# Float64 w_in lands bank by bank in the decoded weights' own buffers, w_out in two landing buffers, under a new step list

## The chip, the cores and the metric

One core of a Trainium2 chip runs the whole program. The time is device microseconds of one execution on that core; the median of several executions counts. PE is the matmul engine, DVE the vector engine, ACT the scalar engine, POOL the GpSimd engine, and SP only issues DMAs.

## What is computed

```python
# attention: B, H, S, D = 4, 8, 768, 48 (r, k, v, w, u in float32)
for t in range(S):
    cur = einsum('bhd,bhe->bhde', u[None] * kt, vt)
    y[:, :, t] = einsum('bhd,bhde->bhe', rt, state + cur)
    state = wt[:, :, :, None] * state + einsum('bhd,bhe->bhde', kt, vt)
x = y.transpose(0, 2, 1, 3).reshape(3072, 384)
# first MoE: w_in (384 x 2048) and w_out (2048 x 384) come in float64
h = x @ w_in
g = h * cos(h)
x2 = g @ w_out
# second MoE: phi (384 x 32), 8 experts w1 (384 x 1024), w2 (1024 x 384), float32
logits = x2 @ phi        # softmax over the tokens for dispatch, over the slots for combine
out = c @ slot_out       # slot_out from 8 experts of 4 slots each
```

## The kernel before

The 3072 tokens are worked in 24 blocks of 128. For each block j, the attention part runs the recurrence in chunks of 64 (loads `lw`, `lk`, `lr`, `lv`, `lz`; transposes `wT`, `kT`, `rT`, `kN` and matmuls `A`, `U`, `y` on PE; the scans `scan` and `sp`, the products `L` and `ks`, the masked copy `mask`, the state steps `z` and `st`, and `xl` on DVE; copies on ACT; `ru` and `D` on POOL). Its result is a block of x, held as a high and a low part. Then `h.t.q` multiplies block t by bank q of w_in (four banks of 512 columns, 9 matmuls each), and `turns`, `rest`, `cos` and `mul` make g from it: `turns` and `cos` on ACT, `rest` and `mul` on DVE. `gT`, `gc` and `l` transpose g and multiply it by w_out @ phi; the softmax steps (`sum` to `es`) follow per pair of blocks. After the last block the eight experts and the output run.

Both float64 weights are decoded on the chip before use. Each is cut in eight pieces of 256 columns or rows, of 768 KB. A piece is loaded by `raw`, and then needs one ACT step (`abs`) and three DVE steps (`d1`, `d2a`, `d2b`, lines 329, 334, 342), which leave a float32 tile. For a piece n of w_in, `whi` (ACT), `wn` (PE, lines 363 and 364) and `wc` (ACT) split it into the high and low part of bank n // 2, in the tile `wu{n // 2}`. For a piece of w_out, `oT`, `oc`, `om`, `pc`, `pT` and `ps` make its part of w_out @ phi.

Before, a piece of w_in lands in one of two buffers of the pool `raw`, except that the first piece is cut in two halves, the second of them landing in the buffer of bank 0. Four pieces of w_out land two by two in the buffers of banks 3 and 2, the other four in the pool `raw`. The decode tiles `a` have two buffers (pool `dec`).

The order is written out by hand in the string `HEAD`: a list of 1,896 steps, `name.argument.argument`. Each engine runs its own instructions in the order of that list, and nothing else moves them; SP too takes the DMAs in that order, so that a load whose buffer is not yet free holds back every load behind it. A step waits only for what it reads and for the buffers that it takes. The tiles that `wT`, `kT`, `rT`, `kN`, `A`, `U`, `y`, `wn`, `oT` and `pT` write in PSUM share three buffers (pool `ps_a`), those of `h` two (pool `ps_h`).

Of the kernel before, what the change touches and what calls it, by code (L numbers as in the profile page):

```python
# [871 lines left out]
wc.0.0 st.1.0 wn.0.1 d2b.o.1 z.1.1 abs.o.0 abs.o.2 rz.1.0 y.0 d1.o.0 st.1.1 wc.0.1 d2a.o.0 sr.2 oT.2 ru.2 oc.2 oT.3 xh.0 oc.3 d2b.o.0 rz.1.1 kT.2
d1.o.2 xl.0 oT.1 ks.2 lv.3 oT.0 sp.2 y.1 abs.i.1 oc.1 d2a.o.2 d1.i.1 oc.0 kN.2 d2b.o.2 wT.3 om.0 wf.3 xh.1 d2a.i.1 xl.1 oT.4 ksn.2 oT.5 oc.4 U.2
d2b.i.1 oc.5 z.2.0 raw.i.3 st.2.0 lw.5 whi.1 abs.i.4 z.2.1 bo.2 rT.2 bs.2 st.2.1 L.2 wn.1.0 wc.1.0 lz.3 d1.i.4 wn.1.1 wc.1.1 d2a.i.4 rz.2.0 oT.7
scan.3 A.2 abs.i.3 d2b.i.4 d1.i.3 lk.3 D.2 mask.2 d2a.i.3 raw.i.6 h.0.0 oc.7 whi.4 wn.4.1 d2b.i.3 rz.2.1 wc.4.1 kT.3 turns.0.0 wn.4.0 lw.4 whi.3 lr.3
pc.0 ru.3 abs.i.6 sr.3 raw.i.5 ks.3 wc.4.0 oT.6 sp.3 oc.6 d1.i.6 wn.3.0 rest.0.0 wc.3.0 wn.3.1 lk.4 d2a.i.6 rT.3 wT.4 d2b.i.6 wc.3.1 L.3 z.3.0 wf.4
whi.6 cos.0.0 h.1.0 abs.i.5 scan.4 pT.0 raw.i.7 turns.1.0 wn.6.1 d1.i.5 wc.6.1 wn.6.0 bo.3 wT.5 mul.0.0 wc.6.0 sr.4 d2a.i.5 h.0.1 abs.i.7 d2b.i.5 sp.4
whi.5 bs.3 lz.2 A.3 ps.0 turns.0.1 lr.4 rz.3.0 y.2 wf.5 D.3 xh.2 om.1 rest.1.0 d1.i.7 kN.3 cos.1.0 mask.3 ksn.3 wn.5.0 rest.0.1 cos.0.1 wc.5.0 wn.5.1
mul.1.0 raw.o.4 gT.0.0 wc.5.1 d2a.i.7 kT.4 xl.2 lz.4 d2b.i.7 mul.0.1 abs.o.4 whi.7 U.3 pc.1 ks.4 ru.4 raw.o.5 st.3.0 h.0.2 wn.7.0 d1.o.4 turns.0.2
z.3.1 gc.0.0 d2a.o.4 wn.7.1 rest.0.2 wc.7.1 st.3.1 h.1.1 rT.4 gT.0.1 cos.0.2 abs.o.5 wc.7.0 scan.5 turns.1.1 d2b.o.4 bo.4 lw.6 oT.8 oc.8 mul.0.2  # L880
rest.1.1 sr.5 kN.4 d1.o.5 h.0.3 bs.4 cos.1.1 L.4 mul.1.1 pT.1 rz.3.1 d2a.o.5 lk.5 ksn.4 gc.0.1 y.3 turns.0.3 h.1.2 rest.0.3 oT.9 xh.3 ps.1 cos.0.3
raw.o.7 lv.4 d2b.o.5 oT.11 gT.0.2 z.4.0 turns.1.2 oc.11 lr.5 oc.9 D.4 xl.3 oT.10 oc.10 A.4 rest.1.2 U.4 mul.0.3 l.0.0 sp.5 l.0.1 st.4.0 mask.4 abs.o.7
lw.7 lr.6 z.4.1 om.2 cos.1.2 pc.2 gc.0.2 raw.o.6 mul.1.2 abs.o.6 h.2.0 ru.5 gT.0.3 rz.4.1 rT.5 gc.0.3 pT.2 d1.o.6 h.1.3 ps.2 rz.4.0 d1.o.7 st.4.1 wT.6
# [120 lines left out]
```

## Time and profile before

| | us |
|---|---|
| median of 3 executions (516.99 to 518.56) | 517.7 |
| the profiled execution | 517.14 |
| its span, first to last instruction | 515.4 |
| PE busy in the span | 481.4 |
| DVE busy | 426.2 |
| ACT busy | 318.7 |
| POOL busy | 100.2 |

The span is what the trace shows; the 1.74 us between it and the execution's own time lie around the program. Busy times are unions over the instructions of an engine. The trace numbers time from the start of the span.

### The profile page before, as it was taken

The numbers are of one execution on the slowest core, as the hardware profiler recorded it, in microseconds if no ns is written. First come the engines' busy times: TensorE is split into PE (matmuls) and PEld (weight loads), VectorE is DVE, ScalarE is ACT, GpSimd is POOL, SyncE is SP. The second block draws the span as 40 slices with busy tenths as digits, with TensorE's granted clock in tenths as the row PEclk, the third lists the DMA queues.
The fourth block names the chain that finished last, engine by engine and source line by source line (L and its number), as shares of the span: only waits on it lengthen the run. The fifth ranks groups of instructions, "written<-read, shape, count | busy, mean of one in ns | idle before, by whom it ended". The sixth has DMA issues, their size and how long they took to land.

```text
span 515.4 us, 15516 instructions
## 1 busy us (share of the span) xinstructions
PE 481.4 (93%) x6515; PEld 378.3 (73%) x6515; DVE 426.2 (83%) x809; ACT 318.7 (62%) x703; POOL 100.2 (19%) x127
## 2 busy tenths in 40 slices
PE   3677899999999999999999999999999999998994
PEld 2445568887888878888877878878788787774573
DVE  4989999998988879999799899899878966674423
ACT  3276687776576676676656766657665756564421
POOL 2431221234212221221114112133120100002200
PEclk9989999999999999999999999999999999999997
DMA  9995968642633315025260341525130891289948
GB/s 208 313 191 139 198 166 203 139 66 45 100 67 68 59 36 93 18 51 76 48 108 4 62 73 23 108 48 95 25 56 17 350 369 39 102 294 336 400 174 269
DMA packets 146325, 67.47 MB, mean 131 GB/s; under 512 B 127184, under 2 KB 134352, under 8 KB 146256
## 3 DMA queue, kind: packets, MB, share of 16 engines
q1 hardware_dynamic: 146256, 66.49, 51.5%
q8 instruction: 51, 0.84, 0.7%
q14 instruction: 18, 0.15, 0.1%
HBM read 61.75 MB, written 4.72 MB: 129 GB/s over the span
## 4 chain that ended last, share of the span: by engine, by line
PE 53%; DVE 7%; ACT 3%; issue 1%
PE h L421 9%; PE h L423 8%; PE h L422 8%; PE gT L455 6%; PE l L470 3%; PE E L566 3%; PE A L193 2%; PE hps L754 2%; PE so L794 2%; PE y L267 2%; PE U L239 1%; DVE g L440 1%; PE o L827 1%; PE rT L134 1%; PE kT L134 1%; DVE lt L214 1%
## 5 line engine op out<-in xcount | busy, mean ns | idle before, releaser
L421 PE MATMUL h<-wu,x 128*128 128x512 f32 x288 | 121.4, 422 | 1.4 <-DVE g L448 1.3
L423 PE MATMUL h<-wu,x 128*128 128x512 f32 x288 | 113.2, 393 | 0.0
L422 PE MATMUL h<-wu,x 128*128 128x512 f32 x288 | 112.6, 391 | 0.0
L444 ACT ACTIVATE g<-g,half_pi 128x512 f32<-128x512 f32 (+1 forms) x97 | 69.2, 719 | 32.2 <-DVE g L440 31.6
L436 ACT ACTIVATE g<-h 128x512 int32<-128x512 f32 (+1 forms) x96 | 56.6, 595 | 51.8 <-PE h L423 41.9
L440 DVE SCALAR_TENSOR_TENSOR g<-g,h 128x512 f32<-128x512 int32 (+1 forms) x96 | 64.5, 675 | 18.0 <-ACT g L436 17.6
L448 DVE TENSOR_TENSOR g<-g,h 128x512 f32<-128x512 f32 (+1 forms) x96 | 64.7, 675 | 13.3 <-ACT g L444 12.3
L207 POOL TENSOR_SCALAR_AFFINE_SELECT lt<-bo 64x512 f32<-64x512 f32 x48 | 37.3, 778 | 159.4 <-ACT bo L230 89.6
L421 PEld LDWEIGHTS h<-wu,x 128*128 128x128 f32 x288 | 54.2, 188 | 16.5 <-issue 3.5
L461 ACT COPY gt<-gT 128x512 f32<-128x512 f32 x89 | 51.8, 585 | 19.1 <-PE gT L455 15.7
L423 PEld LDWEIGHTS h<-wu,x 128*128 128x128 f32 x288 | 54.0, 188 | 12.3
L422 PEld LDWEIGHTS h<-wu,x 128*128 128x128 f32 x288 | 54.4, 189 | 8.7
L455 PE MATMUL gT<-cs,g 128*128 128x128 f32 x384 | 57.5, 275 | 0.2
L162 POOL TENSOR_TENSOR ru<-rn,u_b 128x384 f32<-128x384 f32 x24 | 26.2, 1092 | 133.8 <-DMA rn<-in_r_dram 82.9
L455 PEld LDWEIGHTS gT<-cs,g 128*128 128x128 f32 x384 | 44.7, 141 | 8.2 <-issue 1.9
L214 DVE COPY_PREDICATED lt<-cs,A 64x512 f32<-64x512 uint32 x48 | 35.4, 737 | 1.6 <-POOL lt L207 0.3
L253 ACT COPY rzs<-z 64x192 f32<-64x192 f32 x96 | 33.4, 348 | 4.1 <-DVE z L248 3.0
L149 DVE TENSOR_TENSOR_SCAN qt<-wf,one_b 128x520 f32<-128x520 f32 x24 | 30.4, 1267 | 5.8 <-ACT wf L144 5.7
L178 DVE TENSOR_TENSOR lt<-rT,pt 64x512 f32<-64x512 f32 x48 | 32.8, 683 | 0.8 <-PE rT L134 0.2
L470 PE MATMUL l<-gt,p_sb 128*32 128x128 f32 x768 | 30.7, 276 | 0.3 <-DVE gt L461 0.3
L193 PE MATMUL A<-lt,ks 64*64 64x64 f32 x768 | 28.0, 224 | 3.0 <-DVE st_state L256 1.6
L157 DVE TENSOR_TENSOR_SCAN pt<-wf,ini_f 128x520 f32<-128x520 f32 x24 | 30.1, 1256 | 0.1
(167 smaller groups left out, 782.5 us busy)
## 6 DMA issues: line engine op xcount, KB each, us to landing
we<-in_moe_w_dram SPq DMA_DIRECT2D x16, 1536.0 KB, 9.6
rawi<-in_moe_w_in_dram SPq DMA_DIRECT2D x7, 768.0 KB, 5.0
wn<-in_w_dram SPq DMA_DIRECT2D x24, 192.0 KB, 4.4
kn<-in_k_dram SPq DMA_DIRECT2D x24, 192.0 KB, 4.0
rn<-in_r_dram SPq DMA_DIRECT2D x24, 192.0 KB, 3.9
vn<-in_v_dram SPq DMA_DIRECT2D x24, 192.0 KB, 3.8
...
```

What stands on the lines that cost most here:

```text
L193: nc.tensor.matmul(ps[64 - 64 * a:128 - 64 * a, s, :], lhsT=ks[k, s, :], rhs=L[k, a, s, :], start=True, stop=True)
L214: nc.vector.copy_predicated(out=lt[j % 2][h, a], mask=mask[h].bitcast(U32).unsqueeze(1).to_broadcast([64, NS, C]), data=ps[h])
L421: nc.tensor.matmul(half[:, f], lhsT=xh[:, c, :], rhs=wh, start=(c == 0), stop=False)
L422: nc.tensor.matmul(half[:, f], lhsT=xl[:, c, :], rhs=wh, start=False, stop=False)
L423: nc.tensor.matmul(half[:, f], lhsT=xh[:, c, :], rhs=wl, start=False, stop=(c == KD - 1))
L436: nc.scalar.activation(gt.bitcast(I32), hp, AF.Copy, bias=0.25, scale=1.0 / TWO_PI)
L440: nc.vector.scalar_tensor_tensor(out=gt, in0=gt.bitcast(I32), scalar=-TWO_PI, in1=hp, op0=ALU.mult, op1=ALU.add)
L444: nc.scalar.activation(gt, gt, AF.Sin, bias=half_pi[:, 0:1])
L448: nc.vector.tensor_tensor(out=gt, in0=gt, in1=hp, op=ALU.mult)
L455: nc.tensor.transpose(ps[:, m * 128:(m + 1) * 128], gt[:, m * 128:(m + 1) * 128], ident)
L461: (nc.vector.tensor_copy if n >= ATT and n % 8 in (1, 2, 5) else nc.scalar.copy)(gt_t[t, q], pend.pop(("gT", t, q)))
L470: nc.tensor.matmul(lps_t[g][32 * m:32 * m + 32, o:o + TB], lhsT=p_sb[:, 4 * q + m, :], rhs=gt[:, m * 128:(m + 1) * 128], start=first, stop ...
```

## The change

It does four things. The whole bank q of w_in now lands in the buffer of `wu{q}`, the tile of its decoded halves; the first bank comes as two loads of 256 columns, the other three as one load of 1.5 MB each. Since the decoded halves overwrite the raw bank, the first `whi` of a bank comes after both pieces of the bank have been decoded, and four decode tiles take the place of two. All eight pieces of w_out go through the two buffers of the pool `raw`. The first piece is no longer decoded in halves, which makes one `d1`, `d2a`, `d2b` of 768 columns out of two of 384. And the step list is another one, from its first step to its last.

```diff
-    dec = d_stack.enter_context(tc.tile_pool(name="dec", bufs=2))
+    dec = d_stack.enter_context(tc.tile_pool(name="dec", bufs=4))
...
+    def e_raw(x, n):
         if x == "i":
-            if hf:
-                raw_t[x, n, hf] = wu_p.tile([128, 4 * DM, 2], I32, tag="wu0", name=f"rawi{n}b")[:, 0:768, :]
-            else:
-                raw_t[x, n, hf] = raw_p.tile([128, 768, 2], I32, tag="raw", name=f"rawi{n}")
...
-            nc.sync.dma_start(dst, src)
-        elif n < 4:
-            t = wu_p.tile([128, 4 * DM, 2], I32, tag=f"wu{3 - n // 2}", name=f"rawo{n}")
...
+            q, f = n // 2, slice((n % 2) * 256, (n % 2) * 256 + 256) if n < 2 else slice(0, 512)
+            if q not in rawi_t:
+                rawi_t[q] = wu_p.tile([128, KD * 512, 2], I32, tag=f"wu{q}", name=f"rawi{q}").rearrange("p (k f) t -> p k f t", k=KD)
+            t = rawi_t[q]
+            src = w_in[:, q * 512 + f.start:q * 512 + f.stop].bitcast(I32).rearrange("(k p) f -> p k f", p=128)
+            nc.sync.dma_start(t.rearrange("p k f t -> p k (f t)")[:, :, 2 * f.start:2 * f.stop], src)
+            for i in (n,) if n < 2 else (n, n + 1):
+                raw_t[x, i] = t[:, :, (i % 2) * 256:(i % 2) * 256 + 256, :]
         else:
             t = raw_p.tile([128, 768, 2], I32, tag="raw", name=f"rawo{n}")
...
     def e_whi(n):
-        if n % 2 == 0:
+        if n // 2 not in wu:
             wu[n // 2] = wu_p.tile([128, 2, KD, 512], F32R, tag=f"wu{n // 2}", name=f"wu{n // 2}")
...
-lw.0 lk.0 raw.i.2 z.0.0 wT.0 lw.1 kT.0 wf.0 scan.0 raw.i.0.0 abs.i.2 ks.0 sr.0 sp.0 d1.i.2 d2a.i.2 wT.1 lr.0 misc kN.0 ru.0 wf.1 scan.1 ksn.0 d2b.i.2
+raw.i.0 abs.i.0 raw.i.1 lw.0 d1.i.0 lk.0 abs.i.1 wT.0 raw.i.2 lw.1 d2a.i.0 d2b.i.0 z.0.0 lr.0 d1.i.1 d2a.i.1 d2b.i.1 kT.0 wf.0 whi.1 scan.0 misc ks.0
```

On SP, the first loads of the program now stand like this (`rawi` is a piece or a bank of w_in, `wn`, `kn`, `rn`, `vn` are the loads `lw`, `lk`, `lr`, `lv` of a block; rows with neither sign are in both):

```order
-L999 UNCONDITIONAL_BRANCH
-L607 DMA cs<-in_const_dram 128x320
+L983 UNCONDITIONAL_BRANCH
+L591 DMA cs<-in_const_dram 128x320
+L300 DMA rawi_155<-in_moe_w_in_dram 128x3x512 x2
 L117 DMA wn_121<-in_w_dram 128x8x48
 L117 DMA kn_119<-in_k_dram 128x8x48
-L310 DMA rawi_157<-in_moe_w_in_dram 128x3x512
+L300 DMA rawi_170<-in_moe_w_in_dram 128x3x1024
 L117 DMA wn_122<-in_w_dram 128x8x48
-L310 DMA rawi_175<-in_moe_w_in_dram 128x3x256
 L117 DMA rn_117<-in_r_dram 128x8x48
```

The whole first bank of w_in moved ahead of the loads of block 0, and the whole second bank stands between block 0 and block 1.

On DVE, the rows up to the product `L` of block 4 (the row with two `lt`), before the change:

```order
L149 SCALAR_TENSOR_TENSOR qt_1018<-wf,one_b 128x520
L342 SCALAR_TENSOR_TENSOR wo_sb<-rawo_915,ao_936 128x768
L225 TENSOR_REDUCE bo_1023<-ru_961 128x2x4
L448 TENSOR_TENSOR g_2_981<-g_2_981,h_2_967 128x512
L440 SCALAR_TENSOR_TENSOR g_1_1020<-g_1_1020,h_1_994 128x512
L153 RECIPROCAL ini_f<-qt_1018 128x8
L329 TENSOR_SCALAR ao_1015<-ao_1015 128x768
L178 TENSOR_TENSOR lt_125<-rT_1004,pt_811 64x512 x2
```

And after it (lines 320, 326, 424 and 432 are the 334, 342, 440 and 448 of before):

```order
L326 SCALAR_TENSOR_TENSOR wo_sb<-rawo_900,ao_967 128x768
L225 TENSOR_REDUCE bo_1041<-ru_1036 128x2x4
L157 SCALAR_TENSOR_TENSOR pt_1055<-wf,ini_f 128x520
L285 TENSOR_TENSOR x_115<-y_1003,x_115 128x3x128
L432 TENSOR_TENSOR g_1_995<-g_1_995,h_1_973 128x512
L320 SCALAR_TENSOR_TENSOR ao_858<-rawo_831,ao_858 128x768
L424 SCALAR_TENSOR_TENSOR g_3_1081<-g_3_1081,h_3_1045 128x512
L326 SCALAR_TENSOR_TENSOR wo_sb<-rawo_831,ao_858 128x768
L178 TENSOR_TENSOR lt_125<-rT_1083,pt_1055 64x512 x2
```

The scan of block 5 (`qt_1018`) and its reciprocal have left this place for a later one; `xl` of block 3 (the row with `x_115`), a `mul`, a `rest`, and the `d2a` and `d2b` of piece 5 of w_out have come ahead of it.

On PE, the rows around the matmuls `A` of block 4, which read that `L`, before:

```order
L423 MATMUL h_2_1102<-wu_685,x_115 128x512
L375 MATMUL woT_1113<-cs,wo_sb 128x128 x3
L375 MATMUL woT_1124<-cs,wo_sb 128x128 x3
L455 MATMUL gT_2_1128<-cs,g_2_981 128x128 x4
L375 MATMUL woT_1145<-cs,wo_sb 128x128 x3
L193 MATMUL A_1151<-lt_125,ks_959 64x64 x16
```

And after:

```order
L407 MATMUL h_2_1102<-wu_449,x_115 128x512
L359 MATMUL woT_1124<-cs,wo_sb 128x128 x3
L193 MATMUL A_1135<-lt_125,ks_993 64x64 x16
```

Some transposes of w_out moved from just ahead of `A` to elsewhere; over all rows ahead of it, before has one `oT` more (`oT.10`) and after one `l` more (`l.0.0`), and the rest is the same set in another order.

## Rows read from the trace of the kernel before

**Rows 1.** The page, section 1: busy time and share of each engine.

```profile
PE 481.4 (93%) x6515; PEld 378.3 (73%) x6515; DVE 426.2 (83%) x809; ACT 318.7 (62%) x703; POOL 100.2 (19%) x127
...
PE   3677899999999999999999999999999999998994
```

**Rows 2.** Busy time by stretch, granted clock, DMA share, GB/s, for PE, PEld, DVE, ACT, POOL.

```profile
0.00:70.00 70.00, 48.13 (x504) 33.44 (x506) 61.15 (x90) 38.44 (x75) 19.66 (x35) 0.98 0.90 209
70.00:120.00 50.00, 49.91 (x792) 41.89 (x792) 47.72 (x81) 38.98 (x87) 15.43 (x16) 1.00 0.60 132
120.00:400.00 280.00, 278.52 (x3914) 226.40 (x3907) 251.43 (x493) 183.82 (x416) 57.14 (x64) 1.00 0.34 58
```

**Rows 3.** Timeline of PE: start, length, instruction; in brackets the idle time before it.

```profile
...
21.34 2.04 PE L363 MATMUL wl<-ai,cs 128*128 128x512 f32 x2 [1.59 <-DVE lt L178]
...
23.61 1.05 PE L134 MATMUL kT<-cs,kn 128*128 128x128 f32 x4
...
73.39 1.10 PE L363 MATMUL wl<-ai,cs 128*128 128x512 f32 x2
...
91.27 0.97 PE L193 MATMUL A<-lt,ks 64*64 64x64 f32 x26
...
101.25 0.60 PE L200 MATMUL kN<-cs,ks 128*128 128x128 f32 x4
```

**Rows 4.** Timeline of DVE, the same columns.

```profile
...
6.65 1.24 DVE L149 TENSOR_TENSOR_SCAN qt<-wf,one_b 128x520 f32<-128x520 f32 x1 [5.52 <-ACT wf L144]
...
14.92 0.81 DVE L329 TENSOR_SCALAR ai<-ai 128x384 int32<-128x384 int32 x1
...
18.11 1.78 DVE L248 TENSOR_TENSOR z<-st_state,qt 128x192 f32<-128x192 f32 x1
...
24.27 0.54 DVE L342 SCALAR_TENSOR_TENSOR ai<-rawi0b,ai 128x384 int32<-128x384 int32 x1
24.74 0.54 DVE L225 TENSOR_REDUCE bo<-ru 128x8 f32<-128x384 f32 x1
...
71.72 1.52 DVE L214 COPY_PREDICATED lt<-cs,A 64x512 f32<-64x512 uint32 x2
...
83.12 0.67 DVE L448 TENSOR_TENSOR g<-g,h 128x512 f32<-128x512 f32 x1
83.73 0.69 DVE L440 SCALAR_TENSOR_TENSOR g<-g,h 128x512 f32<-128x512 int32 x1
...
84.88 1.39 DVE L178 TENSOR_TENSOR lt<-rT,pt 64x512 f32<-64x512 f32 x2
...
88.53 0.95 DVE L342 SCALAR_TENSOR_TENSOR wo_sb<-rawo,ao 128x768 int32<-128x768 int32 x1
89.40 0.35 DVE L248 TENSOR_TENSOR z<-st_state,qt 128x192 f32<-128x192 f32 x1
89.67 0.55 DVE L285 TENSOR_TENSOR x<-y,x 128x384 fp32r<-128x384 f32 x1
...
100.36 0.69 DVE L184 TENSOR_TENSOR ks<-kT,qt 128x512 f32<-128x512 f32 x1
```

**Rows 5.** Timeline of POOL, beside the long DVE rows.

```profile
...
14.45 1.00 POOL L163 TENSOR_TENSOR ru<-ru,kn 128x384 f32<-128x384 f32 x1
17.07 1.63 POOL L207 TENSOR_SCALAR_AFFINE_SELECT lt<-bo 64x512 f32<-64x512 f32 x2 [1.62 <-ACT bo L230]
```

**Rows 6.** Timeline of ACT: the first landing of a float64 load.

```profile
...
8.36 0.90 ACT L325 ACTIVATE ai<-rawi 128x768 f32<-128x768 f32 x1 [1.82 <-DMA rawi<-in_moe_w_in_dram]
```

**Rows 7.** Timeline of PE: first matmuls that wait for a load.

```profile
...
4.77 1.09 PE L134 MATMUL wT<-cs,wn 128*128 128x128 f32 x4 [4.77 <-DMA wn<-in_w_dram]
...
9.58 1.09 PE L134 MATMUL wT<-cs,wn 128*128 128x128 f32 x4 [2.79 <-DMA wn<-in_w_dram]
```

**Rows 8.** Short stretches, columns as in Rows 2.

```profile
2.00:4.00 2.00, 0.00 (x0) 0.00 (x0) 0.00 (x0) 0.59 (x3) 1.90 (x8) 1.00 1.01 219
...
24.00:26.00 2.00, 2.00 (x12) 1.56 (x11) 1.88 (x4) 0.89 (x2) 0.00 (x0) 1.00 1.06 358
```

More of the change, by code (lines that the diff above doesn't have):

```diff
@@ L872 @@
[L872 to L883, printed above, removed]
@@ new lines @@
+st.0.1 A.0 raw.i.6 L.1 kT.1 mask.0 wn.2.0 whi.3 rz.0.1 wT.2 lk.2 lr.3 d1.i.4 wc.2.0 wf.2 y.0 ks.1 wn.3.0 d1.i.5 d2a.i.4 d2a.i.5 bo.1 ru.2 wc.3.0
+scan.2 lz.1 lv.1 xh.0 bs.1 z.1.0 D.1 kN.1 d2b.i.5 sr.2 wn.2.1 d2b.i.4 ksn.1 A.1 raw.o.0 wc.2.1 wn.3.1 whi.5 xl.0 abs.i.6 bo.2 lv.2 mask.1 kT.2 sp.2
+abs.i.7 lw.3 h.0.0 whi.4 wn.5.0 d1.i.6 ks.2 wc.3.1 raw.o.1 wn.5.1 rz.1.0 turns.0.0 d1.i.7 d2a.i.6 d2a.i.7 wc.5.0 abs.o.0 bs.2 wc.5.1 U.1 wT.3 st.1.0
+d1.o.0 z.1.1 d2a.o.0 st.1.1 wf.3 kN.2 d2b.o.0 rz.1.1 wn.4.0 lk.3 d2b.i.7 ksn.2 rest.0.0 cos.0.0 rT.2 raw.o.2 L.2 y.1 xh.1 mul.0.0 abs.o.1 z.2.0 h.0.1
@@ new lines @@
+wn.4.1 wc.4.0 xl.1 d2b.i.6 wc.4.1 scan.3 U.2 d1.o.1 oT.0 ru.3 h.1.0 lv.3 rz.2.0 sr.3 st.2.0 oc.0 d2a.o.1 turns.0.1 abs.o.2 whi.6 gT.0.0 oT.1 wn.6.1
+turns.1.0 D.2 oc.1 z.2.1 d2b.o.1 whi.7 st.2.1 d1.o.2 oT.2 wn.6.0 oc.2 wc.6.1 sp.3 lv.4 wc.6.0 lw.4 d2a.o.2 rest.1.0 A.2 d2b.o.2 raw.o.3 oT.3 gc.0.0
+cos.1.0 bo.3 rT.3 oc.3 bs.3 wn.7.0 L.3 om.0 kT.3 mask.2 wc.7.0 D.3 ks.3 abs.o.3 wT.4 wf.4 z.3.0 oT.4 pc.0 lr.4 oT.5 d1.o.3 A.3 oc.4 kN.3 mul.1.0 oc.5
+d2a.o.3 rest.0.1 pT.0 raw.o.5 d2b.o.3 rz.2.1 ksn.3 h.0.2 oT.6 ps.0 oT.7 cos.0.1 abs.o.5 mask.3 lz.2 scan.4 lk.4 oc.6 l.0.0 oc.7 turns.0.2 U.3 lw.5
@@ new lines @@
+st.3.0 raw.o.4 y.2 om.1 rz.3.0 rest.0.2 xh.2 z.3.1 mul.0.1 wn.7.1 lr.5 lz.3 cos.0.2 d1.o.5 pc.1 abs.o.4 st.3.1 mul.0.2 wc.7.1 sr.4 h.1.1 d1.o.4 xl.2
+d2a.o.4 rz.3.1 kT.4 ks.4 turns.1.1 lw.6 gT.0.1 y.3 ru.4 rest.1.1 d2b.o.4 bo.4 pT.1 h.0.3 sp.4 xh.3 oT.9 gc.0.1 cos.1.1 ps.1 gT.0.2 bs.4 kN.4 xl.3
+mul.1.1 lk.5 turns.0.3 rT.4 d2a.o.5 oc.9 wT.5 ksn.4 oT.8 h.1.2 rest.0.3 d2b.o.5 cos.0.3 L.4 gc.0.2 oc.8 raw.o.6 wf.5 oT.11 turns.1.2 oc.11 lr.6 D.4
+A.4 raw.o.7 mul.0.3 rest.1.2 cos.1.2 lz.4 z.4.0 lv.5 U.4 mask.4 st.4.0 abs.o.6 scan.5 gT.0.3 gc.0.3 rz.4.0 z.4.1 h.1.3 oT.10 kT.5 gT.1.1 oc.10 sr.5
@@ L957 @@
+l.23.0 l.22.2 l.22.3 cos.23.1 cos.23.3.1 mul.23.1 gT.23.1 gc.23.2 mul.23.3.1 gT.23.3 gc.23.3 tab gc.23.1 l.23.1 l.23.2 l.23.3 sum.11 we.9 lc.11 E.10.1
+quart.11 max.11 exp.11 dT.11 cmb.0.6 dc.11 ltok.11 E.11.1 we.7 E.11.0 es.10 esl.11.0 esl.11.1 cmb.1.6
 """
```

193 lines of the change are left out of this document (88 added, 105 removed).

## The prediction

> **What bounds the kernel now.** I read the page first: PE is busy 93% of the span, and the slices show where it is not, in the first five and the last four of forty [rows 1]. The busy times by stretch give the missing part in numbers: in the first 70 us PE is idle 21.9 us, in the next 50 us 0.1, from 120 to 400 us 1.5 [rows 2]. All of PE's idle time is 515.4 - 481.4 = 34.0 us, so some 10.6 lie behind 400 us. From 70 us on the kernel is as fast as PE. What can still be won is in the first 70 us, and there DVE is the engine with the work: 61.2 of 70 us, and its first 6.65 us are a wait for the first block's loads [rows 2, 4]. Behind its first row it hardly stops.
>
> Then I looked in the two timelines for the place where PE draws level with DVE. The masked copy of block 3 ends on DVE at 71.72 + 1.52 = 73.24 us, and the `wn` matmul that needs the PSUM buffer it frees starts at 73.39 [rows 3, 4]. Up to here PE takes what DVE gives; from here it has work in stock. So the time of the whole program is set by how early PE can have done a given amount of its work under DVE's deliveries, and everything behind is PE's own pace. The reader should therefore compare the same PE instruction in both orders, with the PE work ahead of it and with the DVE work ahead of what it reads.
>
> **The change at such a place.** I take the matmuls `A` of block 4, which read `L` of block 4. Before, `L` ends at 84.88 + 1.39 = 86.27 us and `A` starts at 91.27 [rows 3, 4]; PE was busy all the while, so it is not `L` that holds `A` here, it is PE's own queue. Ahead of `A` stands the same PE work in both orders (one `oT` less, one `l` more after the change). So if after the change DVE delivers `L` and its neighbours earlier than 91.27, and PE is fed evenly on the way, PE can stand here earlier.
>
> DVE's work ahead of `L`, by start-to-start times, since a DVE instruction starts some 0.08 us before the one ahead of it has ended: a `mul` is 83.73 - 83.12 = 0.61, a `d2b` of 768 columns 89.40 - 88.53 = 0.87, a `d2b` of 384 columns 24.74 - 24.27 = 0.47, `xl` 0.55 - 0.08 = 0.47, `rest` 0.69 - 0.08 = 0.61, a scan 1.24 - 0.08 = 1.16 [rows 4]; `d2a` has the size and form of `d2b`, and a `d1` I take at half of it, since it reads and writes one tensor (0.45; 0.3 for half the columns).
> - Only before: the scan of block 5 with its reciprocal (1.16 + 0.1), and six decode steps of half width: 2 x (0.3 + 0.47 + 0.47) = 2.5. Together 3.8.
> - Only after: three decode steps of full width (0.45 + 2 x 0.87 = 2.2), `xl.3` 0.47, one `mul` and one `rest` 1.2, `d2a` and `d2b` of one piece of w_out 1.7. Together 5.6.
>
> So `L` has 1.8 us more DVE work ahead: 86.27 + 1.8 = 88.1 us, if DVE starts as early and is held up as much as before. Just ahead of `A` stands an `oT` that takes one of the three PSUM buffers, the one that `L` frees; it costs PE 0.3 us. `A` could start at 88.4, which is 2.9 us earlier than before.
>
> **What DVE's start costs.** The decode of the first bank now comes first, and the loads of block 0 stand behind 1.5 MB. One load of 192 KB costs the queue 1.2 us: the 768 KB piece has landed when `abs` starts at 8.36, and the next load's transpose starts at 9.58 [rows 6, 7]. Between the first transpose at 4.77 and 8.36 the queue delivered a load of 192 KB and the 768 KB, so the latter took 2.4 us [rows 6, 7]. The constants, which are ahead of the load that landed at 4.77, are then in at about 3.5. So after the change the two halves of bank 0 land at 5.9 and 8.3, block 0's `wn` at 9.5, `kn` at 10.7, bank 1 (twice 2.4) at 15.5, block 1's `wn` at 16.7, `rn` at 17.9. DVE decodes piece 0 from about 6.9 to 9.1 (`abs` takes 0.90 [rows 6]), piece 1 to 11.3, then come the scan, `ks` and the second scan of block 0, to 14.4. Then it waits for `abs` of bank 1, until 16.4. The scan of block 1 starts at 18.3, `L` and the rest of bank 1's decode last to 24.1. The state step behind them waits for `U` on PE, which stands behind three `wn` blocks: 2.3 us for the large one (21.34 to 23.61 [rows 3]), about 1 each for two of half its columns, 1 for `U`, from `whi` at 18.5 on: 23.8 to 24.2. So this step ends at 24.5. The DVE work up to it is 15.1 us (four decoded pieces 8.8, two scans and one of the second kind 3.5, `L` 1.4, five small steps 1.4), and before DVE had done as much at about 24.1, just ahead of the row at 24.27 [rows 4]. The start costs **0.4 us**, with bounds 0 (the waits cover it) and 5 (next part).
>
> **What POOL costs.** Some DVE instructions take far longer than their kind: the `d1` of half width at 14.92 took 0.81, the `z` at 18.11 1.78 against 0.35 at 89.40, while `ru` ran on POOL from 14.45 to 15.45 and `D` from 17.07 to 18.70 [rows 4, 5]. Six such rows up to 67 us add some 4.5 us, over seven `ru` or `D`. In the walk above only one `ru` has run by 24.5 us, before it was two `ru` and one `D` by then; so one or two of them still come, at 0 to 0.8 each. I take **0.4** together, bounds 0 and 1.6. The Trainium skill (SBUF — State Buffer, SBUF: two separate sides) says that a DVE instruction with two SBUF inputs or in a two-port mode and a reading GpSimd instruction hold one port pair exclusively, and the loser waits for the whole instruction. These rows agree for the `d1` (0.81, with `ru` still running). By that rule alone the two late ones could cost a whole instruction each, 2 us together, and the gain would shrink to some 0.5.
>
> **The sum.** At `A` of block 4: 2.9 - 0.4 - 0.4 = 2.1 us earlier. A second place as a check: `kN` of block 5 started at 101.25, behind its `ks`, which ended at 100.36 + 0.69 = 101.05 [rows 3, 4]. After the change `ks` has 2.1 us less DVE work ahead (no `L` of block 5, no sixth `d1` of w_out's last piece, the halves saved), and PE 0.3 us less; 2.1 - 0.8 - 0.3 leaves 1.0. But DVE had by then waited for PE's own results, which come earlier too, so the truth lies between, nearer the first: **1.8 us**. Nothing behind adds to it: PE's and DVE's instructions are the same set in another order, the tail is the same code, and the loads of the experts still start when the last block's `y` is done. The four decode tiles and the landing in place cost nothing by themselves: they are the same `abs`, `d1`, `d2a`, `d2b`; `whi` waits for two pieces in place of one, which is in the walk. The profiled execution would take 517.14 - 1.8 = 515.3; the median, 0.6 above the profiled one, **515.9 us**.
>
> **Rivals.**
> - *The gain is eaten (517.3 us).* DVE is level with PE over a long stretch. Any wait that the new order puts on DVE or on PE there comes off the gain, and the 1.5 us of small waits from 120 to 400 us [rows 2] may as well be 3. For it: the second place leaves but 1.0. Against it: `L` and `A` differ by 2.9 before the deductions.
> - *The loads come too late (519.5 us).* DVE has only 7.4 us of work ahead of bank 1's first `d1`: two pieces, two scans and `ks`. In the first 2 to 4 us the queue moved 219 GB/s, with large rows 358 [rows 8]. At 219 GB/s the 3.7 MB up to the end of bank 1 take 17 us, it lands at 19 (no load moves before 2 us), `d1` starts at 20 in place of 16.4, and `U`'s chain and everything behind moves by some 3.6: 515.9 + 3.6 = 519.5. It decides from a landing of bank 1 at 17.3 us on, where the whole gain is gone, and the kernel is over 0.3% slower from 18.9. Against it: the 768 KB took 2.4 us here, 328 GB/s. The Trainium skill (DMA: Bandwidth & Descriptors, Queues, rings and completion order) says that each DMA engine takes the descriptors of a queue's ring in order; so the loads of block 0 cannot pass the bank ahead of them. The landings at 8.36 and 9.58, in order of issue, agree.
> - *More is won (513.5 us).* If the late POOL rows fall beside nothing, and DVE's long rows halve (2.2 of 4.5 us), the gain is 1.8 + 0.4 + 2.2 = 4.4.
>
> **How the numbers follow.** I give my forecast 0.44, the eaten gain 0.29, the late loads 0.21, the larger gain 0.06. A measurement of this kernel tells about 0.3%, 1.55 us, from no change. Faster by that is my forecast, mostly, and the larger gain: 0.47; within it the eaten gain and a margin: 0.31; slower 0.22. The range reaches from the larger gain to the late loads: 513.4 to 519.6; the forecast's own is 514.4 to 516.6.
>
> **What would show it.** In the profile after: DVE's first decode row at about 6.9 and its first scan near 11.3; the first `d1` of bank 1 near 16.4; the first `st_state` near 24.2; `L` of block 4 ending near 89 and `A` behind it at once; PE idle in the first 70 us near 20 in place of 21.9, though the first `h` stands earlier. I am wrong if `d1` of bank 1 starts behind 18, if PE waits for DVE behind 100 us, or if POOL holds DVE longer than the 4.5 us of before.

## The result, and the profile after

The changed kernel took 522.67 us (median of 4 runs, 521.56 to 523.53) beside 517.35 of the kernel before: ratio 1.0102, interval 1.0085 to 1.0118. It is 1.0% slower, where the prediction had 515.9. Two more measurements, among the experiments below, gave 1.0071 (1.0047 to 1.0094) and 1.0068 (1.0044 to 1.0092). The profiled execution has a span of 519.9 us, 4.5 more than before; I follow that span first.

The first rows to read are those of the start, which the prediction had walked through: SP (loads issued), ACT and DVE, in the timeline of the changed kernel. Columns as in [rows 3].

```profile
1.25 5.96 SPq L300 DMA_DIRECT2D rawi<-in_moe_w_in_dram  x2
7.26 0.49 SPq L117 DMA_DIRECT2D wn<-in_w_dram  x1
...
8.42 2.87 SPq L300 DMA_DIRECT2D rawi<-in_moe_w_in_dram  x1
...
5.93 0.89 ACT L311 ACTIVATE ai<-rawi 128x768 f32<-128x768 f32 x1 [2.50 <-DMA rawi<-in_moe_w_in_dram]
11.63 0.90 ACT L311 ACTIVATE ai<-rawi 128x768 f32<-128x768 f32 x1 [4.81 <-DMA rawi<-in_moe_w_in_dram]
...
17.91 1.72 ACT L311 ACTIVATE ai<-rawi 128x768 f32<-128x768 f32 x2 [0.69 <-DMA rawi<-in_moe_w_in_dram]
...
6.86 0.56 DVE L315 TENSOR_SCALAR ai<-ai 128x768 int32<-128x768 int32 x1 [6.86 <-ACT ai L311]
11.74 0.96 DVE L320 SCALAR_TENSOR_TENSOR ai<-rawi,ai 128x768 int32<-128x768 int32 x1 [4.32 <-DMA rawi<-in_moe_w_in_dram]
...
16.22 1.23 DVE L149 TENSOR_TENSOR_SCAN qt<-wf,one_b 128x520 f32<-128x520 f32 x1
...
19.55 0.54 DVE L315 TENSOR_SCALAR ai<-ai 128x768 int32<-128x768 int32 x1
...
28.82 0.36 DVE L256 TENSOR_TENSOR st_state<-U,z 128x192 f32<-128x192 f32 x1
```

Piece 0 lands at 5.93, as predicted (5.9), and its `d1` runs at 6.86 (6.9). Then two things stop. SP's pair of `rawi` loads takes 5.96 us, until 7.21 (the same pair takes 0.95 in e1 below); 5.2 of them are a wait of SP for ACT, and the loads behind the pair leave 5.0 us (`wn` of block 0) to 3.2 us (from `wn` of block 1 on) later than there. And DVE's `d2a` of piece 0, whose data are there, waits 4.32 us, for the *second* piece. The first scan starts at 16.22 in place of 11.3, `d1` of bank 1 at 19.55 in place of 16.4, the first `st_state` ends at 29.18 in place of 24.5. The queue is not short of bandwidth, it runs empty: its share is 0.97 from 4 to 5 us and 0.03 from 7 to 8, and 0.46 in the first row below (0.88 before).

By stretch, columns as in [rows 2] (PE's and DVE's busy time are the first and third pair):

```profile
0.00:10.00 10.00, 0.00 (x0) 0.00 (x0) 0.56 (x1) 2.69 (x4) 3.31 (x21) 1.00 0.46 146
10.00:20.00 10.00, 5.75 (x18) 3.80 (x19) 8.02 (x11) 4.04 (x5) 0.00 (x0) 1.00 1.18 286
70.00:100.00 30.00, 29.17 (x451) 24.32 (x450) 29.81 (x49) 22.10 (x50) 4.97 (x5) 1.00 0.71 165
100.00:120.00 20.00, 19.25 (x287) 16.30 (x287) 17.76 (x32) 15.11 (x37) 5.60 (x6) 1.00 0.46 76
120.00:160.00 40.00, 38.55 (x554) 31.15 (x553) 36.59 (x64) 23.94 (x56) 10.17 (x11) 1.00 0.38 70
...
200.00:400.00 200.00, 199.65 (x2828) 163.27 (x2821) 180.45 (x351) 133.65 (x299) 42.37 (x48) 1.00 0.32 57
470.00:475.00 5.00, 3.59 (x33) 1.51 (x33) 1.80 (x7) 0.88 (x5) 0.29 (x1) 0.66 0.07 26
```

From 70 to 160 us PE is idle 0.83 + 0.75 + 1.45 = 3.0 us, where the kernel before had at most 0.1 from 70 to 120 [rows 2] and 0.1 from 120 to 160 (39.91 of 40 busy). From 200 to 400 it wins 0.8 back (1.1 idle before). The waits are small, each for DVE or ACT: 0.2 to 0.8 us; the largest stands just ahead of `A` of block 4. In the first 70 us PE is idle 4.0 us more than before (44.16 us busy against 48.13 [rows 2]). These sum to more than the delay, since PE's busy time is 478.2 us for the same 6515 matmuls that took 481.4 [rows 1], which nothing in the rows explains. At the last `l` PE stands 2.3 us behind the kernel before (465.91 against 463.61).

At `A` of block 4, the place for which the prediction made its sum, the changed kernel stands where the kernel before stood: 91.34 beside 91.27, in place of the forecast 89.2 (timeline of the changed kernel, DVE and PE).

```profile
90.21 1.40 DVE L178 TENSOR_TENSOR lt<-rT,pt 64x512 f32<-64x512 f32 x2
...
91.34 1.29 PE L193 MATMUL A<-lt,ks 64*64 64x64 f32 x27
```

So of the 4.5 us in the profile 0.1 is lost up to there, 2.2 from there to the last `l`, and 2.2 behind it.

The 2.2 us behind it go in the code that the prediction called the same. The last softmax group, first of the kernel before, then of the changed kernel (PE, DVE and ACT rows of the timeline):

```profile
465.02 0.70 PE L483 MATMUL lc<-lg,cs 128*128 128x256 f32 x2 [0.55 <-DVE lg L477]
465.76 0.42 DVE L491 TENSOR_REDUCE mx<-lc 128x1 f32<-128x256 f32 x1 [0.79 <-PE lc L483]
466.22 0.85 ACT L502 COPY dl<-lc 32x64 f32<-32x64 f32 x4 [0.81 <-DVE mx L491]
467.59 0.33 PE L540 MATMUL dT<-cs,dl 128*128 128x128 f32 x1 [0.88 <-ACT dl L512]
468.43 1.93 PE L566 MATMUL E<-g,dt 128*32 128x256 f32 x32 [0.51 <-ACT dt L547]
469.63 0.48 DVE L572 SCALAR_TENSOR_TENSOR e_sb<-e_sb,al,E 128x256 f32<-128x256 f32 x1 [1.97 <-PE E L566]
470.39 0.35 PE L722 MATMUL sum<-st_s,cs 128*128 128x1 f32 x2
```

```profile
467.32 0.70 PE L467 MATMUL lc<-lg,cs 128*128 128x256 f32 x2 [0.55 <-DVE lg L461]
468.05 0.85 ACT L486 COPY dl<-lc 32x64 f32<-32x64 f32 x4 [0.35 <-PE lc L467]
468.94 0.42 DVE L475 TENSOR_REDUCE mx<-lc 128x1 f32<-128x256 f32 x1 [1.67 <-ACT dl L486]
470.34 0.33 PE L524 MATMUL dT<-cs,dl 128*128 128x128 f32 x1 [1.32 <-ACT dl L496]
471.18 3.27 PE L550 MATMUL E<-g,dt 128*32 128x256 f32 x32 [0.51 <-ACT dt L531]
474.54 0.48 DVE L556 SCALAR_TENSOR_TENSOR e_sb<-e_sb,al,E 128x256 f32<-128x256 f32 x1 [2.03 <-PE E L550]
475.30 0.35 PE L706 MATMUL sum<-st_s,cs 128*128 128x1 f32 x2 [0.86 <-DVE st_s L558]
```

From `lc`, the matmul that gathers the group's logits in PSUM, to `sum`, which adds up the sums `st_s`, it takes 5.37 us before and 7.98 after; 0.4 of these 2.6 us come back behind `sum`. Three things differ. The step list has `quart.11 max.11` in place of `max.11 quart.11`: four copies on ACT now go ahead of the maximum on DVE, both of which read `lc`, and `dT` comes 0.45 us later. It has `E.11.1` ahead of `E.11.0`: the first `e_sb` row of 256 columns, behind which `st_s` is updated, needs `E.11.0`, so it no longer starts when half of `E` is done (469.63, `E` ending at 470.36) but behind all of it (474.54), and `sum` waits 0.86 us for `st_s`. And the same `E` matmuls took 3.27 us instead of 1.93, at a granted clock of 0.66 on average over 470 to 475 us (part of it at 1.2 GHz; 1.00 before). The Trainium skill (PSUM — Partial Sum Buffer, PSUM bank collisions raise a hardware error) says that two engines may not read one bank and quadrant at once and that software must order them. The rows agree: in either order the second reader starts 0.04 us behind the end of the first, so the list decides which of the two is late.

### The profile page after: what moved, and what is told of

Read it like the earlier page. It is cut to its first block, busy times and chain, and to the rows that moved or that the text cites. A ratio compares the mean times of both kernels' runs of the same rounds, so it can differ in the third digit from the quotient of the medians.

```text
span 519.9 us, 15529 instructions
## 1 busy us (share of the span) xinstructions
PE 478.2 (92%) x6515; PEld 377.5 (73%) x6515; DVE 425.1 (82%) x806; ACT 318.0 (61%) x702; POOL 101.4 (19%) x127
## 4 chain that ended last, share of the span: by engine, by line
PE 70%; DVE 20%; ACT 3%; issue 3%; DMA 2%; POOL 0%; SPq 0%; ACTq 0%; DVEq 0%; POOLq 0%
PE h L405 11%; PE h L407 11%; PE h L406 11%; PE gT L439 7%; PE l L454 4%; PE E L550 4%; PE A L193 3%; PE y L267 3%; PE hps L738 2%; PE so L778 2%; PE U L239 2%; DMA rawi<-in_moe_w_in_dram 2%; DVE qt L149 2%; DVE lt L178 1%; DVE g L432 1%
## 5 line engine op out<-in xcount | busy, mean ns | idle before, releaser
L207 POOL TENSOR_SCALAR_AFFINE_SELECT lt<-bo 64x512 f32<-64x512 f32 x48 | 40.3, 839 | 201.6 <-ACT bo L230 160.2
L445 ACT COPY gt<-gT 128x512 f32<-128x512 f32 x89 | 51.6, 582 | 14.7 <-PE gT L439 9.3
L454 PE MATMUL l<-gt,p_sb 128*32 128x128 f32 x768 | 32.4, 277 | 0.3 <-DVE gt L445 0.3
```

The lines of the kernel that those rows point to most:

```text
L445: (nc.vector.tensor_copy if n >= ATT and n % 8 in (1, 2, 5) else nc.scalar.copy)(gt_t[t, q], pend.pop(("gT", t, q)))
L454: nc.tensor.matmul(lps_t[g][32 * m:32 * m + 32, o:o + TB], lhsT=p_sb[:, 4 * q + m, :], rhs=gt[:, m * 128:(m + 1) * 128], start=first, stop ...
```

## Experiments

Theory 1, the false wait: the pieces of bank 0 land in one tile, interleaved by rows, so the stretch of the tile from the first to the last element of one load overlaps that of the other. The program's dependencies then take the two as one: the load of piece 1 waits for `abs` of piece 0 on ACT, and `d2a` of piece 0 for both loads. The list of instructions with their waits shows both (SP's rows first, then DVE's):

```
2 L300 DMA rawi_155<-in_moe_w_in_dram 128x3x512
3 L300 DMA rawi_155<-in_moe_w_in_dram 128x3x512 [waits Activation_49]
...
2 L320 SCALAR_TENSOR_TENSOR ai_157<-rawi_155,ai_157 128x768 [waits DMAHW2_49,DMAHW1_49,DVE_49]
```

So a step here waits for a buffer by whole stretches of a tile, not by the parts that it touches. Theory 2: the order itself, block 0's loads behind bank 0. Theory 3: the end alone. Every ratio is to the kernel before, measured beside it.

| run | edit to the changed kernel | median us | ratio | interval |
|---|---|---|---|---|
| e8 | none | 522.31 | 1.0071 | 1.0047 to 1.0094 |
| e1 | split landing | 517.17 | 1.0010 | 0.9987 to 1.0033 |
| e2 | second load ahead of `abs` | 521.25 | 1.0073 | 1.0056 to 1.0090 |
| e3 | end as before | 520.27 | 1.0052 | 1.0033 to 1.0070 |
| e4 | block 0's loads first | 524.77 | 1.0133 | 1.0112 to 1.0154 |
| e5 | split landing, end as before | 516.57 | 0.9969 | 0.9948 to 0.9990 |
| e6 | one pair of the end exchanged | 520.81 | 1.0053 | 1.0027 to 1.0079 |
| e7 | kernel before, with the changed end | 518.97 | 1.0019 | 1.0001 to 1.0037 |
| e9 | e5, half of `ru` left out | 514.73 | 0.9953 | 0.9938 to 0.9967 |
| e10 | e5, block 0 first, `wf` behind `abs` | 526.81 | 1.0184 | 1.0162 to 1.0205 |
| e11 | e5, block 0 first | 517.17 | 1.0008 | 0.9987 to 1.0028 |
| e12 | e1, SP's wait put back | 521.35 | 1.0076 | 1.0048 to 1.0103 |
| e13 | half of `ru` left out | 518.34 | 1.0014 | 0.9998 to 1.0030 |
| e14 | none | 521.66 | 1.0068 | 1.0044 to 1.0092 |

**e1, split landing.**

```diff
-                rawi_t[q] = wu_p.tile([128, KD * 512, 2], I32, tag=f"wu{q}", name=f"rawi{q}").rearrange("p (k f) t -> p k f t", k=KD)
+                rawi_t[q] = wu_p.tile([128, KD * 512, 2], I32, tag=f"wu{q}", name=f"rawi{q}")
+                rawi_t[q] = rawi_t[q].rearrange("p (h k f) t -> p h k f t", h=2, k=KD) if q == 0 else rawi_t[q].rearrange("p (k f) t -> p k f t", k=KD)
...
+            if n < 2:
+                raw_t[x, n] = t[:, n]
+                nc.sync.dma_start(t[:, n].rearrange("p k f t -> p k (f t)"), src)
+                return
```

> The two pieces of bank 0 land in the two halves of the same buffer, each half in one piece, instead of interleaved by rows; nothing else differs from the changed kernel. Theory 1 (false wait: the second piece's load waits for abs of the first, and d2a of the first for both pieces): the two loads go out back to back, d2a of piece 0 starts near 7.5 us instead of 11.74, the first scan near 12 instead of 16.2, d1 of bank 1 near 16 instead of 19.55, and the kernel takes 518 to 519.5 us, 3 to 4.5 less than the changed kernel's 522.7. Theory 2 (the order itself: loads of block 0 stand behind bank 0): the wait goes, but the time stays within 1 us of 522.7. Theory 3 (the end of the program alone): the end still takes 54 us from the last l wait, and at most 2.3 us come back in front of it.

Both waits are gone, and the time is that of the kernel before: theory 1, with a median below its forecast of 518 to 519.5. By the ratios it is 3.2 us less than the changed kernel (e8). The timeline of e1 (SP, DVE and PE):

```profile
1.25 0.95 SPq L303 DMA_DIRECT2D rawi<-in_moe_w_in_dram  x2
...
7.81 0.96 DVE L325 SCALAR_TENSOR_TENSOR ai<-rawi,ai 128x768 int32<-128x768 int32 x1
...
12.29 1.23 DVE L149 TENSOR_TENSOR_SCAN qt<-wf,one_b 128x520 f32<-128x520 f32 x1
...
15.69 0.56 DVE L320 TENSOR_SCALAR ai<-ai 128x768 int32<-128x768 int32 x1
...
84.89 1.40 DVE L178 TENSOR_TENSOR lt<-rT,pt 64x512 f32<-64x512 f32 x2
...
85.53 0.55 PE L364 MATMUL woT<-cs,wo_sb 128*128 128x128 f32 x3 [0.82 <-ACT wt L370]
86.02 1.30 PE L193 MATMUL A<-lt,ks 64*64 64x64 f32 x27
```

`L` of block 4 now stands where it stood in the kernel before (84.89 beside 84.88 [rows 4]), 5.3 us earlier than in the changed kernel. `A` comes right behind it, 5.3 us earlier than in the kernel before (91.27 [rows 3]), and the last `lc` 2.6 earlier (462.39 against 465.02): half of the lead is lost on the way, where PE is idle 3.5 us from 70 to 160 us, and nearly all of the rest in the end (8.32 us from `lc` to `sum`).

**e2, the second load ahead of abs.** The list begins `raw.i.0 raw.i.1 abs.i.0`.

> The step list begins raw.i.0 raw.i.1 abs.i.0 instead of raw.i.0 abs.i.0 raw.i.1: SP no longer waits for ACT, but abs and d2a of piece 0 still wait for both pieces. Theory 1: the pieces land by about 8.5 us, decode of piece 0 starts near 9 instead of 11.7, the loads behind leave 4 us earlier, and the time is 518.5 to 520, at most 1 us above the split landing. Theory 2: within 1 us of 522.7. Theory 3: at most 2.3 us come back.

SP's wait is gone, DVE's is not: `d1` of piece 0 starts at 9.67, the scan at 14.73. The time is above what theory 1 forecast: 1.0073, no better than e8. The rows are those of its fastest execution (519.04; the other six took 521.1 to 522.1).

**e12, SP's wait alone.** On e1, a small transfer that needs `abs` of piece 0 stands on SP's queue ahead of the second load.

```diff
+            if n == 1:
+                nc.scalar.copy(hold[0], a_t["i", 0][:, 0:1])
+                nc.sync.dma_start(hold[1], hold[0])
```

> The split landing with the end as in the changed kernel, and a wait of SP put back by itself: a 512-byte transfer that needs abs of piece 0 stands on SP's queue ahead of the second piece's load, while DVE and ACT may decode piece 0 alone. The piece in front of the queue's wait is decoded from 6.9 us on, but piece 1 and everything behind leave SP 5 us later. If SP's wait is the larger part of the false wait, this costs 3.5 to 5 us against the split landing (517.2): 521 to 522.5, as much as the changed kernel itself, though the exchanged steps (SP free, DVE and ACT waiting for both pieces) had won but 1.4. If the waits of DVE and ACT are the larger part, it is within 1.5 us of the split landing.

1.0076, as the first of the two cases has it: piece 0 is decoded from 6.96 on, then DVE waits 3.64 us for piece 1 and scans at 15.82. With e2: either half of the false wait, by itself, costs what both cost together, as far as the intervals tell (each time is known to 0.9 to 1.4 us). For e12 the rows say why: DVE needs both pieces before the scan, which starts but 0.4 us earlier than in the changed kernel (piece 1 is 0.8 later here, its `abs` at 12.43 in place of 11.63). In e2 the scan starts 1.5 us earlier, and why none of that is left in the time is not shown.

**e4, block 0's loads first.** The list begins `lw.0 lk.0 raw.i.0 abs.i.0 raw.i.1`.

> The step list begins lw.0 lk.0 raw.i.0 abs.i.0 raw.i.1: decay and keys of block 0 go out before bank 0, the false wait stays. Theory 2 (block 0 waits for its loads behind bank 0): first scan near 10 us, 6 earlier than in the changed kernel, and the time 518 to 519.5. Theory 1 (the loads behind the waiting second piece, bank 1 above all, are what DVE lacks): wT comes early, but d1 of bank 1 stays at 19 or later, and no more than 2 us come back (520.7 to 522.7).

Slower than the changed kernel by 0.3 to 0.7%. `wT` has its data early (it starts at 4.85), but DVE's list has the decode ahead of the scan, and all of the decode is 2.07 us later (`d2a` of piece 0 at 13.81, scan at 18.28). Theory 2 forecast 518 to 519.5 and fails; but since the scan still stood behind the decode, it is e11 below that tests the order itself.

**e3, the end as before.**

```diff
-l.23.1 l.23.2 l.23.3 sum.11 we.9 lc.11 E.10.1 quart.11 max.11 exp.11 dT.11 cmb.0.6 dc.11 ltok.11 E.11.1 we.7 E.11.0 es.10 esl.11.0 esl.11.1 cmb.1.6
+we.9 we.7 cmb.0.6 cmb.1.6 l.23.1 l.23.2 l.23.3 sum.11 lc.11 E.10.1 max.11 quart.11 exp.11 dT.11 dc.11 es.10 E.11.0 E.11.1 esl.11.0 esl.11.1 ltok.11
```

> The changed kernel with its last 21 steps in the order of the kernel before (we.9, we.7, cmb.0.6 and cmb.1.6 moved ahead of l.23.1, E.11.0 ahead of E.11.1, es.10 ahead of both). Theory 3 (2.2 of the 5.3 us are lost in the end): the stretch from the last wait of l to the end takes 51.8 us again and the time is 520.5. Theories 1 and 2 alone: the end is slower because of the clock, not of the order, and the time stays at 522 to 523.

From `lc` to `sum` it takes 5.37 us again, and the time falls to 520.27. **e7** puts the changed end on the kernel before (so `cmb.0.6`, `cmb.1.6`, `we.9` and `we.7` move behind `l.23.1` from places farther ahead):

> The kernel before with the changed kernel's last 21 steps (we.9, we.7, cmb.0.6, cmb.1.6 moved behind l.23.1, quart.11 ahead of max.11, E.11.1 ahead of E.11.0, es.10 late). If the end is a loss of its own, independent of the start, this is slower than the kernel before by 2.2 us (1.3 of order, 1 to 1.5 of granted clock where it falls): 519 to 520, ratio 1.003 to 1.005. If the end of the changed kernel is slow for what happens ahead of it, the time stays at 517 to 518.

1.0019: slower by some 1.0 us, less than forecast; from `lc` to `sum` 6.62 us in its profile, 1.25 more than before, with the clock at 1.00 throughout; 0.3 of it comes back behind `sum` (44.69 us to the end, 45.01 before), which leaves 0.9. **e6** exchanges `quart.11` and `max.11` alone:

> The changed kernel with one pair of steps exchanged: max.11 ahead of quart.11, as before the change. If the end is slow because the four copies on ACT hold up the maximum on DVE (both read the PSUM tile lc), dT of the last group comes some 1.0 us earlier after lc than in the changed kernel (2.0 to 2.2 behind the end of lc in place of 3.0) and the time falls by 1.0 to 521.7; if TensorE's granted clock then stays at 1.00 in the last E matmuls, by up to 2.4. If the order of the other steps (E.11.1 ahead of E.11.0, es.10 last, cmb behind) is the cause, less than 0.5 comes back.

`dT` comes 0.44 us earlier behind `lc`, so the second case: `sum` still waits 0.88 for `st_s`, and `lc` to `sum` is 6.23. The pair is worth 0.4 us of the end's order, the late `E.11.0` the other 0.9 by `sum`'s wait (no run moves that step alone); I had sized the pair at 1.0, by the whole length of the copies, where DVE's maximum had always cost ACT half of that. The time, 1.0053, can't be told from e8's. The clock is the third part: of the nine profiles with the changed end it fell in five (e1, e4, e8, e14 and the changed kernel, `E` 2.99 to 3.62 us), and stayed in four (e2, e7, e12, e13, `E` 1.93). It never fell in the six with the old end. That e6, too, kept it is one profile, and proves nothing.

**e5, both edits.**

> Both edits on the changed kernel: bank 0 lands in two separate halves, and the last 21 steps are in the order of the kernel before. If the false wait and the end are two separate losses, the times add: 2.6 us earlier than the kernel before at the last l wait, as in the split landing alone, and an end of 51.8 us; 514 to 515.5 us, ratio to before 0.994 to 0.997. If the end's loss comes back only because the program stands later, or the gain of the start is eaten in the end by the expert weights' loads, 516.5 to 518.

0.9969: faster than both kernels by an interval that ends at 0.9990. The losses are two, and within the noise they add: against e8, the split landing alone wins 3.2 us, the end alone 1.0, both 5.3, each known to some 1.6 us. **e8** is the changed kernel once more:

> The changed kernel once more, unaltered, beside the others on one chip: 522 to 523, and the end at a granted clock that may differ from run to run.

**e9, POOL's part.** On e5, `ru` is one product in place of two (the factor `u` is left out).

```diff
-        nc.gpsimd.tensor_tensor(out=ru, in0=rn[j % 2][:, :, 0:D], in1=u_b, op=ALU.mult)
-        nc.gpsimd.tensor_tensor(out=ru, in0=ru, in1=kn[j % 2][:, :, 0:D], op=ALU.mult)
+        nc.gpsimd.tensor_tensor(out=ru, in0=rn[j % 2][:, :, 0:D], in1=kn[j % 2][:, :, 0:D], op=ALU.mult)
```

> The kernel with both edits (split landing, end as before), and POOL's ru in one product instead of two: it leaves out the factor u, so ru is r times k. POOL then runs 24 instructions of about 1 us less, 5 of them in the first 90 us. If POOL's hold on DVE is on the path that sets the end (the stretched DVE rows of the first 91 us add some 6 us), a third to a half of that goes: 1.5 to 3 us less than the kernel with both edits (516.6), 513.5 to 515. If DVE makes up for the holds while it waits for PE and loads, less than 0.7 us comes back.

0.9953 against 0.9969: some 0.8 us, near the second case. The intervals overlap, so it may be nothing, or 2; it isn't 3 us. **e13** makes the same edit on the changed kernel, with **e14**, the changed kernel, beside it:

> The changed kernel with POOL's ru in one product instead of two (the factor u is left out). If the holds of the changed kernel (5.2 to 5.9 us of held rows in most profiles, 2.7 before) are a loss of their own, the held rows fall to 3 or less and the time by 1.5 to 3 us against e14: 519.3 to 520.8. If the false wait and the end are all, no more comes back than between e5 and e9, 0.8 us: 521.5 or more.

> The changed kernel, unaltered, beside e13 on one chip: 522 to 523, ratio 1.007 to 1.010; held rows of 5 to 6 us in most executions.

Here it wins 1.0068 - 1.0014 = 0.54%, 2.8 us, as the first case has it for the time, but not for the rows. The held rows, DVE's rows from 20 to 90 us that are more than 0.35 us longer than the shortest of their form, still add 5.0 us in e13's profile (4.3 in e14), and `A` of block 4 starts at 91.67, 0.8 later than in e14. The two profiles are 3.0 us apart in span: 0.6 at the last `l` (464.83 and 465.46; PE is idle 0.87 us from 120 to 160 us in e13 and 1.65 in e14), 1.0 from there to `sum`, where `E` takes 1.93 us and 2.99, and 1.3 behind `sum`. The last part shows in the matmuls `si` (timeline of PE, e13 and then e14):

```profile
474.21 3.07 PE L718 MATMUL si<-wo_sb,et 128*32 128x256 f32 x64 [0.29 <-ACT et L709]
```

```profile
476.17 4.01 PE L719 MATMUL si<-wo_sb,et 128*32 128x256 f32 x64
```

The granted clock is 0.64 from 470 to 475 us and 0.67 from 475 to 480 in e14, and 1.00 in both stretches in e13. So of what separates these two profiles 2.4 us come with the lower clock in the end, and 0.6 lie ahead of it. Half of `ru` costs the changed kernel some 2.8 us and e5 some 0.8, and what it costs is not where I had looked.

**e10 and e11, block 0 ahead of bank 0 again, on e5.**

> The kernel with both edits, and at the very start block 0 ahead of bank 0 again: its two loads first, and its scan, ks and second scan ahead of the decode on DVE. Without the false wait nothing stands between the loads, so bank 0's pieces land some 2.4 us later than in the split landing (near 8.5 and 10.8), when DVE's scans of block 0 (6.65 to 10.0) are over. If only the false wait and the end were wrong with the change, this is as good as the split landing with bank 0 first, within 0.7 us (516 to 517.2). If the decode of bank 0 ahead of block 0 is itself a loss, it is 1 to 2 us faster (514.5 to 515.5); if block 0's loads ahead of bank 0 are a loss, as they were with the false wait in place (2.1 us), it is 518 or more.

526.81, the third case by its number, but not by its mechanism. My list put `wf` of block 0 behind both `abs` on ACT, and the rows show what that does (timeline of e10, ACT and DVE):

```profile
10.25 0.89 ACT L316 ACTIVATE ai<-rawi 128x768 f32<-128x768 f32 x1 [1.10 <-DMA rawi<-in_moe_w_in_dram]
11.04 0.58 ACT L144 COPY wf<-wT 128x512 f32<-128x512 f32 x1
...
11.72 1.24 DVE L149 TENSOR_TENSOR_SCAN qt<-wf,one_b 128x520 f32<-128x520 f32 x1 [10.60 <-ACT wf L144]
```

`wT` was done at 5.8, but the copy that the scan needs waited behind two that waited for a load. It is the same kind of loss as the false wait, and says nothing of the order of the loads. e11 puts `wf` ahead of `abs`, and `kN` ahead of the first `wn`:

> The kernel with both edits and block 0 ahead of bank 0 once more, now with wf of block 0 ahead of abs on ACT and kN of block 0 ahead of the first wn on PE, so that no instruction of block 0 stands behind one that waits for bank 0. DVE should start its first scan near 6.7 us, as the kernel before did, be through with block 0 at 10.0, decode bank 0 from there without a wait, and reach d1 of bank 1 near 16.4, where that bank has landed. If the start is bound by bank 1's landing, this is equal to the kernel with both edits within 0.7 us (515.8 to 517.2; ratio 0.994 to 0.999). If the decode of bank 0 first is itself a loss it is 1 to 2 us faster (ratio 0.991 to 0.995). If the loads' order alone was what made the two earlier tries slow, it is over 518.

1.0008: outside the first case by its ratio, some 2 us slower than e5, and between the cases. DVE starts its scan at 6.51 and never waits for bank 0, but then waits 1.74 us for bank 1 and starts its `d1` at 16.57 (15.69 in e1, 17.39 in e5). The decode of bank 0 first is no loss: DVE is held at bank 1 in either order. Here block 0 does come first, on SP and on DVE, and nothing is won: theory 2 falls.

## Why the prediction was wrong

**The failed step is "What DVE's start costs".** It gave 0.4 us (bounds 0 and 5) on a walk in which "the two halves of bank 0 land at 5.9 and 8.3". The first landed at 5.93. The second was not issued until ACT had read the first, and DVE would not go on with the first until the second was there. DVE's first state step ended 4.7 us later than the walk had it, and at `A` of block 4 the whole lead of 2.1 us was gone (91.34); without the false wait, in e1, `A` stands at 86.02. The term measured 3.2 to 4.3 us in the time: 1.0071 to 1.0010 with the changed end, 1.0052 to 0.9969 with the old one. That lies within the bounds, but these were drawn for another mechanism, the bytes. The row that showed it stood in the order with its waits, not in any trace of before; I had priced the loads by bytes and queue order and had not asked what each load must wait for. Of the three signs that I had named for being wrong, the first (`d1` of bank 1 behind 18) came true at 19.55, and the second (PE waiting for DVE behind 100 us) by five waits of 0.2 to 0.55 us between 100 and 130 us.

**"Nothing behind adds to it ... the tail is the same code" failed too.** The tail is the same instructions in another order: 1.3 us of order from `lc` to `sum`, of which 0.3 to 0.4 come back behind `sum`, and 1.1 to 1.7 more in the profiles where the clock fell (in e14 another 1.3 behind `sum`); 1.0 us in the time by e7, 1.0 to 2.1 by e3 and e5.

**The rivals.** *Loads come too late* gave 519.5 and named the right place and the sign: bank 1 was in at 17.9 (its `abs`), behind the 17.3 from which the gain was to be gone. Its mechanism, 219 GB/s, was wrong: with back-to-back issue bank 1 was in at 14.7, 15.2 and 16.5 (e1, e9, e5), around my 15.5 and not at 19. *The gain is eaten* was right as a mechanism: PE's small waits from 70 to 400 us grew from 1.6 to 3.7 us, in e1 to 4.3. *More is won* has a slip in its sum: 517.7 less 4.4 is 513.3, not 513.5.

**What agreed, in part by luck.** What the order is worth without its two accidents is 0.31% by e5, 1.6 us (0.5 to 2.7 by the interval); the prediction had 1.8. `A` of block 4, forecast 2.1 us earlier, stands at 89.05 in e5, 2.2 earlier, and at 89.25 in e9. But their first state step ends at 26.25 and 25.22, 1.8 and 0.7 us later than in the walk; in e1, where it ends as walked (24.14), `A` is 5.3 earlier. So the walk's start and the lead behind it were both off, in opposite directions. In e1 DVE has the 1.8 us more work ahead of `L` that I had summed, and 2.3 us less of the held rows of the next paragraph (2.4, before 4.7), so `L` stands where it stood before. That the time of e5 comes near the forecast is a sum of such differences, not a proof of its terms.

**"What POOL costs" is a spread.** The prediction took 0.4 (bounds 0 and 1.6) over what POOL cost before, which by its own count of six rows was 4.5 us. Two of these six lie ahead of 20 us, so the held rows of e13, counted from 20 us on, are 2.7 before, and from the start 4.7. The order of the changed kernel has none ahead of 20 us: 5.9 in its profile, 5.4 in e8, 5.2 in e6, 4.3 in e14, but 2.4 in e3, which is the same program up to the end. Against the 4.7 of before that runs from 2.3 less to 1.2 more, and the 0.4 lies in between. e3 and e8 start alike (first scan at 16.19 and 16.25) and have `L` of block 4 at 88.18 and 90.97: 2.8 apart, by the 3.0 of held rows, and the last `l` at 464.30 and 467.15, as far apart still (the profiled execution of e3 is its fastest, 517.75 where the median is 520.27). The first of them, e3 and then e8 (timelines of DVE and POOL):

```profile
20.97 0.55 DVE L315 TENSOR_SCALAR ai<-ai 128x768 int32<-128x768 int32 x1
21.44 1.23 DVE L149 TENSOR_TENSOR_SCAN qt<-wf,one_b 128x520 f32<-128x520 f32 x1
...
21.88 1.59 POOL L162 TENSOR_TENSOR ru<-rn,u_b 128x384 f32<-128x384 f32 x1 [17.93 <-DMA u_b<-in_u_dram]
```

```profile
21.04 1.37 DVE L315 TENSOR_SCALAR ai<-ai 128x768 int32<-128x768 int32 x1
22.32 2.03 DVE L149 TENSOR_TENSOR_SCAN qt<-wf,one_b 128x520 f32<-128x520 f32 x1
...
20.81 1.17 POOL L162 TENSOR_TENSOR ru<-rn,u_b 128x384 f32<-128x384 f32 x1 [16.85 <-DMA u_b<-in_u_dram]
22.06 1.19 POOL L163 TENSOR_TENSOR ru<-ru,kn 128x384 f32<-128x384 f32 x1
```

`u_b` landed 1.07 us earlier in e8, so that the two products of `ru` ran beside `d1` and the scan, which took 0.8 us longer each than in e3; in e3 the second product ran beside `L`, which kept its length, and a `d2a`, which took 0.4 longer than its kind. The sign that I named, more than the 4.5 us of before, came true in three of five profiles of this order (e14 has 4.3). In this pair the held rows are the difference; that they are the loss of the changed kernel is not shown: e13 wins 2.8 us by halving `ru` and has 5.0 us of them.

**Open.** The split landing wins 3.2 us with the changed end, half of `ru` wins 2.8 with the false wait and the changed end in place, and some 0.8 with neither. Whether the first two win the same time is not shown: in the one pair of profiles 2.4 of 3.0 us come with the clock in the end, which never fell in the profiles with the old end, that of e5 and e9. Profiles of several executions each would tell; what decides whether the clock falls there is open too.
